# The half form of the attention step for two more chunks, loaded through the batch loader

## The chip, the cores and the metric

The kernel runs on one core of a Trainium2 chip. The metric is device time in microseconds of one execution. Three runs of the kernel before gave 206.95, 206.97 and 208.53 us; their median is 206.97.

The engines by the names of the profile: PE is TensorE (matmuls; PEld its weight loads), DVE is VectorE, ACT is ScalarE, POOL is GpSimd, SP is the engine that issues most DMAs here. Each executes its own instructions in order.

## The reference, cut to what matters

A recurrence of retention, 4 batches, 8 heads, 768 steps, head size 64, and behind it a feed-forward layer:

```python
# q, k, v: (4, 8, 768, 64); gamma[h] = 1 - 2**(-5-h); scale = 1/8
state = gamma * state + outer(k[t], v[t])
y[t]  = scale * q[t] @ state
x     = y as (3072, 512)            # tokens x (head, dim)
h     = maximum(x @ w_in, 0)        # w_in:  512 x 2048
out   = (h * h) @ w_out             # w_out: 2048 x 512
```

## The kernel before, in words

The 768 steps of a batch are cut into six chunks of 128, so there are 24 chunks, numbered m = 0 to 23; chunk 6 is the first of batch 1. Inside a chunk the recurrence is a masked product of scores, and between chunks a 64 x 64 state for each head is carried. The decay is put into q and k (or v) as powers of gamma, so that the mask is only a triangle.

The feed-forward layer takes the chunks in blocks: block 0 is chunks 0 to 3, then come ten blocks of two chunks. For a block, the first product (L803) makes 16 slices of h, ScalarE takes the relu (L812), and VectorE or ScalarE squares it; the second product is done with seven half-size products in place of eight (L837; for blocks 0 and 1 partly at L1096, and plainly at L1002). Block 2 needs the attention output of chunk 6 at place 51 and that of chunk 7 at place 55; block 3 begins at place 67.

TensorE's instruction stream is a list of "pieces" of the feed-forward work, each about 0.8 us, and before piece n the attention work that was `put` at place n is emitted. Places 16 to 31 are the plain second products of chunks 0 and 1 and the first products of block 1; places 32 to 50 the half-size products of chunks 2 and 3 and of block 1, seven matmuls a place; places 51 to 66 are block 2, and each later block has 16 places. Every engine's order follows from this list, that of the DMA queues on SP and POOL too.

There are three forms of the attention step. Chunks 0 to 3 use a form for pairs. The **full form** (`attend`, chunks 4 to 7 before) scales k by VectorE (`scale_k`), casts v on POOL (`cast_v`, L385), transposes q and k on TensorE (L399, L412) with copies out of PSUM on ScalarE (L405, L419), makes scores of 128 x 128 (L440) that VectorE masks (L447), a state (L479), and outputs (L508, L516). The **half form** (`attend2`, from chunk `PACK_FROM` on) lays a chunk out as two halves of 64 steps, the even heads on partitions 0 to 63 and the odd heads on 64 to 127. POOL casts k into a tile with zeros off the diagonal (`cast_k2`, L658, two instructions of 64 partitions). VectorE scales v by the decay (`scale_v2`, L667), and POOL copies it, again in two instructions, into a second tile with zeros off the diagonal (L675). q and k are transposed by DMA from SP (L425 for the q of two chunks, L681 for each k). The scores are eight matmuls of 64 columns (L697) with one mask on VectorE (L704); each half makes a state (L724), copied to SBUF by two ScalarE instructions (L733, L734); the outputs are up to 16 matmuls of 64 columns (L746, L753). The tiles `ks_bd2s` and `v_bd2s` are two each, and chunks take them in turn; `kT` tiles are two as well.

Loads: `load_q` (L105) brings the q of two chunks in one 512 KB DMA from SP. `load_kv` (L124) brings k or v of one chunk in one 256 KB DMA from SP with all 128 partitions. `batch_loads` (L147) is a generator that brings k or v of a batch in the layout of the half form, one DMA for each half of the partitions and each of four head pairs: 128 KB each on SP for chunks 8 to 11, 96 KB each (three chunks) on POOL for the later batches. All DMAs of SP go through one queue, and each waits for the one eight before it. The weights w_out are loaded and cast by POOL's DMAs (L171).

`attend2(m, d, before, q_at, qturn_at, k_at, turn_at, v_at)` puts the steps of a chunk: states at d-6 and d-3, scores at d-5, outputs at d; the others at the places given, for later chunks d-19, d-16, d-18, d-13 and d-9. `pack_constants` makes the decay table and the mask of the half form in two steps, and `zero_off_diagonal` clears tiles once on POOL.

Of the kernel before, what the change touches and what calls it, by code (L numbers as in the profile page):

```python
# [21 lines left out]

PACK_FROM = 8


@with_exitstack
def kernel(
# [9 lines left out]
    nc = tc.nc  # L39
# [13 lines left out]
    NCHUNK = len(chunks)  # L53
# [79 lines left out]
    def batch_loads(m, name, size):  # L133


        b, i = chunks[m]
        src, to = (k, raw_k) if name == "k" else (v, raw_v)
        t = kept_tiles.pop((m, name), None)
        if t is None:
            t = stage_tile(2 * NCH * NPAIR * D)  # L140
        t = t.rearrange("s (p w d) -> s p w d", p=NPAIR, d=D)
        for j in range(NCH - i):
            to[m + j] = t[:, :, 2 * j : 2 * j + 2].rearrange("s p u d -> s u p d")
        for w in range(0, NCH - i, size):
            for hh, rows in enumerate(halves):
                for p in range(NPAIR):
                    (nc.sync if m == 8 else nc.gpsimd).dma_start(  # L147
                        t[rows, p, 2 * w : 2 * (w + size)],
                        src[b, 2 * p + hh, (i + w) * C : (i + w + size) * C].rearrange(
                            "(w s) d -> s w d", s=64  # L150
                        ),
                    )
                    yield
# [41 lines left out]
    def exponents(pattern, step, name, logs, parts=(slice(0, P),)):  # L195
        ex_i = const.tile([P, NCH, H], I32, name=f"{name}_i")
        for rows in parts:
            nc.gpsimd.iota(ex_i[rows], pattern=pattern, base=0, channel_multiplier=step)

        def scaled():  # L200
            ex_f = const.tile([P, NCH, H], FP32, name=f"{name}_f")
            nc.vector.tensor_copy(ex_f[:], ex_i[:])
            nc.vector.tensor_tensor(
                out=ex_f[:],
                in0=ex_f[:],
                in1=logs[:, None, :].to_broadcast([P, NCH, H]),
                op=ALU.mult,
            )
            return ex_f

        return scaled
# [52 lines left out]
    def pack_constants():  # L264
        lng2 = const.tile([P, 2, NPAIR], FP32)
        for hh, rows in enumerate(halves):
            for p in range(NPAIR):
                nc.gpsimd.memset(lng2[rows, :, p : p + 1], float(np.log(gammas[2 * p + hh])))
        logs = lng2.rearrange("s u p -> s (u p)")
        scaled = exponents([[C, NCH], [C // 2, 2], [0, NPAIR]], 1, "ex_k2", logs, halves)  # L270
        nc.gpsimd.memset(cmask2[:], 0.0)
        for rows in halves:
            nc.gpsimd.affine_select(
                out=cmask2[rows],
                in_=cmask2[rows],
                compare_op=ALU.is_gt,
                fill=1.0,
                base=0,
                pattern=[[-1, 2], [-2, C // 4]],
                channel_multiplier=1,  # L280
            )
# [77 lines left out]
    at = {m: {} for m in range(NCHUNK)}  # L359
# [303 lines left out]
    def scale_v2(m):  # L663
        b, i = chunks[m]
        vn = raw_v.pop(m)
        v2 = v2pool.tile([P, 2 * NPAIR, D], BF16, name="v2")
        nc.vector.tensor_tensor(  # L667
            out=v2.rearrange("s (u p) d -> s u p d", u=2),
            in0=vn,
            in1=kf2[:, i, :, :, None].to_broadcast([P, 2, NPAIR, D]),  # L670
            op=ALU.mult,
        )
        v_bd = v_bd2s[m % 2]
        for hh, rows in enumerate(halves):
            nc.gpsimd.tensor_copy(v_bd[rows, :, hh, :], v2[rows])  # L675
        at[m].update(v2=v2, v_bd=v_bd)

    def transpose_k2(m):
        a = at[m]
# [535 lines left out]
    def put(place, what, *args):  # L1215
        parts.setdefault(place, []).append((what, args))
# [16 lines left out]

    def attend2(m, d, before, q_at, qturn_at, k_at, turn_at, v_at):
        if m % 2 == 0:
            put(q_at, scale_q, m, 0)
            put(q_at + 1, scale_q, m, 1)
            put(qturn_at, dma_transpose_q, m)
        put(k_at, cast_k2, m)
        put(v_at, scale_v2, m)  # L1240
        put(turn_at, transpose_k2, m)
        put(max(d - 6, before), state2, m, 0)
        put(d - 5, scores2, m)
        put(d - 3, state2, m, 1)
        put(d, outputs2, m)
# [7 lines left out]
    put(13, load_w_out, 1)  # L1253
    put(17, load_q, 6)
    attend(5, None, None, 17, 18, 18, (20, 21), 21, 23)
    for m, name in ((6, "k"), (6, "v"), (7, "k"), (7, "v")):
        put(18, load_kv, m, name)
    put(19, load_q, 8)
    put(19, load_w_out, 2)
    put(19, load_w_out, 3)  # L1260
    attend(6, (31, 32), 34, 33, 34, 35, (38, 39), 39, 42)
    attend(7, None, None, 37, 38, 40, (43, 44), 44, 47)

    def early_at(tb, c0, place, begin_at, at_places):
        held = []
# [18 lines left out]
    early_at(1, 0, 3, 32, (34, 34, 35, 36))  # L1284
    for place, tb, which in ((47, 0, 1), (49, 0, 0), (50, 1, 1), (52, 1, 0)):
        put(place, early_store, tb, which)
    packed = pack_constants()
    put(22, next, packed)
    put(38, next, packed)
    for j, t in enumerate(ks_bd2s + v_bd2s + [s_bds[2]]):  # L1290
        for hh in range(2):
            put(24 + j, zero_off_diagonal, t, hh)

    put(37, load_q, 10)
    done = [57, 62] + [70 + 8 * j for j in range(14)]

    ahead = {
        8: (36, 40, 43, 44, 47), 9: (0, 0, 45, 46, 53), 10: (50, 54, 55, 57, 60), 11: (0, 0, 60, 63, 68)
    }
    for m, d in zip(range(PACK_FROM, NCHUNK), done):  # L1300
# [70 lines left out]
```

## Time and profile before

| what | before |
|---|---|
| median of three runs | 206.97 us |
| time of the profiled execution | 208.36 us |
| its span, first to last instruction | 206.6 us |
| granted TensorE clock, mean | 0.998 |
| mean DMA rate over the span | 185 GB/s |
| q1 (DMAs from SP), share of 16 engines' span | 68.4% |
| q0 (DMAs from POOL), share | 19.2% |
| kT transposes (L681): count, us to landing, min / median / max | 16, 3.1 / 4.9 / 9.5 |
| qT transposes (L425): count, us to landing, min / median / max | 8, 3.3 / 5.8 / 9.3 |

An engine's busy time in the profile is the sum of its instructions; a line with "idle before" names who ended the wait. "SPq" is SP as an issuer of DMAs: its entry lasts as long as the issuing takes, which grows when the queue is full. The time to landing is counted from the issue. In the rows of digits, the span is cut into 40 slices of 5.2 us, and a digit is the busy share in tenths.

### The profile page before, as it was taken

The page shows a single profiled execution, that of the slowest core. Times are in us where ns is not written, and L with a number is a line of the kernel's source. Part 1 is how long each engine was busy: PE and PEld are TensorE (multiplying, and loading weights), DVE is VectorE, ACT ScalarE, POOL GpSimd, SP SyncE. Part 2 cuts the span into 40 slices and gives each one's busy share as a digit, 9 for nine tenths or more (in the row PEclk, how much of TensorE's full clock was granted, in tenths as well). Part 3 has the DMA queues.
Part 4 walks back from the last instruction along what each step waited for, and adds up shares of the span by engine and source line. Part 5 has one row for each costly group of instructions (what it writes and reads, how often), then busy time and mean ns, then how long its engine had stood idle before and what let it go on. Part 6 is the DMA issues. An engine that isn't in the chain of part 4 may idle for free.

```text
span 206.6 us, 5855 instructions
## 1 busy us (share of the span) xinstructions
PE 196.7 (95%) x2373; PEld 165.2 (80%) x2373; DVE 152.9 (74%) x305; ACT 135.6 (66%) x276; POOL 112.1 (54%) x198
## 2 busy tenths in 40 slices
PE   5889999999999999999999899999999999999993
PEld 1457644876888998789989699999989999898883
DVE  4687899498885678589697588598697797474374
ACT  8375885677943666693794595793785786874730
POOL 5332549823230768975999788779986226100000
PEclk9999999999999999999999999999999999999999
DMA  6999999999999999899699998799897551300202
GB/s 160 290 313 379 310 268 247 205 203 239 238 169 174 240 292 134 149 289 185 174 200 180 221 225 176 190 197 158 217 201 156 137 105 38 119 0 3 102 0 102
DMA packets 70730, 38.12 MB, mean 185 GB/s; under 512 B 43952, under 2 KB 64688, under 8 KB 70704
## 3 DMA queue, kind: packets, MB, share of 16 engines
q1 hardware_dynamic: 65520, 29.37, 68.4%
q0 software_dynamic: 5184, 8.39, 19.2%
q8 instruction: 18, 0.29, 0.6%
q14 instruction: 8, 0.07, 0.1%
HBM read 27.26 MB, written 6.29 MB: 162 GB/s over the span
## 4 chain that ended last, share of the span: by engine, by line
PE 69%; DMA 17%; POOL 4%; DVE 4%; ACT 2%; issue 1%; SPq 0%; DVEq 0%; ACTq 0%
PE psf L803 28%; PE psf L837 12%; PE tp L837 8%; DMA kT<-ks_bdp 7%; PE psf L1096 6%; DMA stage<-in_moe_w_in_dram 4%; DMA w_out_bf<-in_moe_w_out_dram 3%; PE psf L1002 3%; DMA kn<-in_k_dram 3%; POOL stage L147 2%; PE st L697 2%; POOL ks_bdp L658 2%; PE y L753 1%; PE y L746 1%; PE c_ps L724 1%
## 5 line engine op out<-in xcount | busy, mean ns | idle before, releaser
L803 PE MATMUL psf<-xt,w_in_bf 128*128 128x256 bf16 (+2 forms) x880 | 92.5, 259 | 0.4 <-DVE w_in_bf L336 0.3
L803 PEld LDWEIGHTS <-w_in_bf 128*128 128x128 bf16 x880 | 70.9, 98 | 11.2 <-DVE w_in_bf L336 0.7
L812 ACT ACTIVATE h<-psf 128x512 bf16<-128x512 f32 x96 | 56.2, 595 | 20.5 <-PE psf L803 20.0
L774 DVE TENSOR_TENSOR h<-h 128x512 bf16<-128x512 bf16 x72 | 31.8, 458 | 14.8 <-ACT h L812 14.6
L658 POOL CAST ks_bdp<-stage 64x512 bf16<-64x512 f32 x32 | 25.6, 799 | 20.6 <-issue 12.1
L675 POOL COPY v_bd<-v 64x512 bf16<-64x512 bf16 x32 | 20.6, 642 | 23.4 <-DVE v L667 22.2
L837 PEld LDWEIGHTS <-h 128*128 128x128 bf16 x288 | 26.3, 98 | 3.3 <-DVE h L774 0.6
L833 DVE TENSOR_TENSOR osb<-psf,u 128x256 f32<-128x256 f32 x34 | 13.7, 422 | 17.1 <-ACT u L878 9.9
L147 POOL DMA_DIRECT2D stage<-in_k_dram x32 | 21.0, 662 | 0.0
L147 POOL DMA_DIRECT2D stage<-in_v_dram x32 | 21.0, 662 | 0.0
L760 ACT ACTIVATE xt<-y 128x512 bf16<-128x512 f32 x16 | 12.0, 748 | 8.8 <-PE y L753 8.8
L366 DVE TENSOR_TENSOR qs<-qn,qf 128x512 bf16<-128x512 f32 x22 | 16.6, 758 | 1.1 <-DMA qn<-in_q_dram 1.1
L837 PEld LDWEIGHTS <-k_bd 128*128 128x128 bf16 x144 | 13.7, 98 | 1.8 <-issue 0.2
L772 ACT ACTIVATE h<-h 128x512 bf16<-128x512 bf16 x24 | 14.6, 626 | 0.5
L667 DVE TENSOR_TENSOR v<-stage,kf 128x512 bf16<-128x512 f32 x16 | 13.4, 838 | 0.0
L733 ACT ACTIVATE s_bd<-c_ps 64x256 bf16<-64x256 f32 x29 | 10.6, 367 | 3.4 <-PE c_ps L724 3.3
L704 DVE TENSOR_TENSOR pt<-st,cmask 128x512 bf16<-128x512 f32 x16 | 11.0, 687 | 2.4 <-PE st L697 1.9
L734 ACT ACTIVATE s_bd<-c_ps 64x256 bf16<-64x256 f32 x29 | 11.0, 378 | 0.4
L837 PE MATMUL tp<-w_out_bf,h 128*128 128x256 bf16 x72 | 11.2, 273 | 0.0
L334 POOL CAST w_in_bf<-stage 128x256 bf16<-128x256 f32 x14 | 6.1, 465 | 9.2 <-DMA stage<-in_moe_w_in_dram 9.2
L837 PE MATMUL psf<-w_sum,h 128*128 128x256 bf16 x72 | 10.8, 273 | 0.0
L833 DVE TENSOR_TENSOR k_bd<-h 128x512 bf16<-128x512 bf16 x18 | 10.4, 576 | 0.3
(146 smaller groups left out, 328.7 us busy)
## 6 DMA issues: line engine op xcount, KB each, us to landing
qn<-in_q_dram SPq DMA_DIRECT2D x12, 512.0 KB, 7.0
out_dram<-osb SPq DMA_DIRECT2D x23, 256.0 KB, 3.3
stage<-in_k_dram POOLq DMA_DIRECT2D x32, 96.0 KB, 4.5
stage<-in_v_dram POOLq DMA_DIRECT2D x32, 96.0 KB, 4.9
stage<-in_moe_w_in_dram SPq DMA_DIRECT2D x4, 512.0 KB, 6.9
stage<-in_moe_w_in_dram SPq DMA_DIRECT2D x2, 1024.0 KB, 10.9
w_out_bf<-in_moe_w_out_dram POOLq DMA_DIRECT2D x4, 512.0 KB, 9.5
kn<-in_k_dram SPq DMA_DIRECT2D x2, 512.0 KB, 6.4
```

The costliest lines, as they stand in the source:

```text
L147: (nc.sync if m == 8 else nc.gpsimd).dma_start(t[rows, p, 2 * w : 2 * (w + size)], src[b, 2 * p + hh, (i + w) * C : (i + w + size) * C].re ...
L366: engine.tensor_tensor(out=out, in0=by, in1=table[:, :, None].to_broadcast([P, H, D]), op=ALU.mult)
L658: nc.gpsimd.tensor_copy(ks[rows, :, hh, :].rearrange("s (u p) d -> s u p d", u=2), kn[rows])
L667: nc.vector.tensor_tensor(out=v2.rearrange("s (u p) d -> s u p d", u=2), in0=vn, in1=kf2[:, i, :, :, None].to_broadcast([P, 2, NPAIR, D]), ...
L675: nc.gpsimd.tensor_copy(v_bd[rows, :, hh, :], v2[rows])
L772: nc.scalar.activation(hv, hv, AF.Square)
L774: nc.vector.tensor_mul(hv, hv, hv)
L803: nc.tensor.matmul(hp, lhsT=w_in_bf[g][:, cb, fq * 128 : (fq + 1) * 128], rhs=xts[tb][:, cb, cols], start=(cb == 0), stop=(cb == NCB - 1),)
L812: nc.scalar.activation(hv, hp[:], AF.Relu)
L833: nc.vector.tensor_tensor(out=out, in0=in0, in1=in1, op=op)
L837: nc.tensor.matmul(to, lhsT=left[:, j], rhs=right(j) if callable(right) else right[:, j], start=(start and j == 0), stop=(stop and j == NF ...
L1096: nc.tensor.matmul(to[:], lhsT=left(j), rhs=right(j), start=(start and j == 0), stop=(j == NFB // 2 - 1), skip_group_check=True,)
```

## The change

Chunks 6 and 7 take the half form: `PACK_FROM` goes from 8 to 6, and their two `attend` calls and four `load_kv` are dropped. The k and v of chunks 6 to 11 now all come through `batch_loads` in 96 KB DMAs on SP, chunks 6 to 8 at places 18 to 21 and chunks 9 to 11 at places 32 to 40. The load of q for chunk 8 moves from place 19 to 24, that of 10 from 37 to 36. Constants and cleared tiles of the half form are made sooner. In `attend2` the POOL copies of v are a step of their own, one place behind the scaling, and the transposes of k go from d-13 to d-15. Some loads of chunks 12 to 17 on POOL are a few places later.

On SP the order up to chunk 9 is after the change: q of 6; eight k loads; eight v loads; q of 8; qT of 6; two output stores; kT of 6; eight k loads; q of 10; kT of 7; six v loads; qT of 8; two v loads; kT of 8; an output store; kT of 9. Before it was: q of 6; k, v of 6; k, v of 7; q of 8; five k loads; two output stores; three k loads; eight v loads; q of 10; qT of 8; kT of 8; kT of 9. For the later blocks SP's order is the same in both.

```diff
-PACK_FROM = 8
+PACK_FROM = 6
...
-                    (nc.sync if m == 8 else nc.gpsimd).dma_start(
+                    (nc.sync if m == PACK_FROM else nc.gpsimd).dma_start(
...
+        at[m]["v2"] = v2
+
+    def copy_v2(m):
         v_bd = v_bd2s[m % 2]
         for hh, rows in enumerate(halves):
-            nc.gpsimd.tensor_copy(v_bd[rows, :, hh, :], v2[rows])
-        at[m].update(v2=v2, v_bd=v_bd)
+            nc.gpsimd.tensor_copy(v_bd[rows, :, hh, :], at[m]["v2"][rows])
+        at[m]["v_bd"] = v_bd
...
         put(v_at, scale_v2, m)
+        put(v_at + 1, copy_v2, m)
...
-    for m, name in ((6, "k"), (6, "v"), (7, "k"), (7, "v")):
-        put(18, load_kv, m, name)
-    put(19, load_q, 8)
...
-    attend(6, (31, 32), 34, 33, 34, 35, (38, 39), 39, 42)
-    attend(7, None, None, 37, 38, 40, (43, 44), 44, 47)
...
+    put(24, load_q, 8)
     packed = pack_constants()
     put(22, next, packed)
-    put(38, next, packed)
+    put(27, next, packed)
     for j, t in enumerate(ks_bd2s + v_bd2s + [s_bds[2]]):
         for hh in range(2):
-            put(24 + j, zero_off_diagonal, t, hh)
-
-    put(37, load_q, 10)
-    done = [57, 62] + [70 + 8 * j for j in range(14)]
+            put(20 + j, zero_off_diagonal, t, hh)
+
+    put(36, load_q, 10)
+    done = [44, 49, 57, 62] + [70 + 8 * j for j in range(14)]
     ahead = {
-        8: (36, 40, 43, 44, 47), 9: (0, 0, 45, 46, 53), 10: (50, 54, 55, 57, 60), 11: (0, 0, 60, 63, 68)
+        6: (25, 28, 30, 32, 34), 7: (0, 0, 34, 36, 39),
+        8: (36, 40, 43, 44, 47), 9: (0, 0, 47, 48, 53), 10: (50, 53, 55, 56, 60), 11: (0, 0, 60, 63, 68)
     }
...
-                *ahead.get(m, (d - 19, d - 16, d - 18, d - 13, d - 9)))
+                *ahead.get(m, (d - 19, d - 16, d - 18, d - 15, d - 9)))
...
-        (8, "k"): [23, 23, 24, 24, 25, 32, 32, 33],
-        (8, "v"): [33, 33, 34, 34, 35, 35, 36, 36],
-        (12, "k"): [49, 50, 51, 52, 53, 54, 55, 56] + [74 + j for j in range(8)],
-        (12, "v"): [58, 59, 60, 61, 62, 64, 65, 66] + [82 + j for j in range(8)],
+        (6, "k"): [18 + j // 4 for j in range(8)] + [32 + j // 2 for j in range(8)],
+        (6, "v"): [20 + j // 4 for j in range(8)] + [37 + j // 2 for j in range(8)],
+        (12, "k"): [49, 50, 51, 52, 57, 58, 59, 60] + [74 + j for j in range(8)],
+        (12, "v"): [61, 62, 63, 64, 65, 66, 67, 68] + [82 + j for j in range(8)],
...
-        loads = batch_loads(m, name, 4 if m == 8 else 3)
+        loads = batch_loads(m, name, 3)
```

More of the change, by code (lines that the diff above doesn't have):

```diff
@@ L1286 @@
         put(place, early_store, tb, which)
+    put(24, load_q, 8)
     packed = pack_constants()
     put(22, next, packed)
-    put(38, next, packed)
+    put(27, next, packed)
     for j, t in enumerate(ks_bd2s + v_bd2s + [s_bds[2]]):
         for hh in range(2):
-            put(24 + j, zero_off_diagonal, t, hh)
-    put(37, load_q, 10)
-    done = [57, 62] + [70 + 8 * j for j in range(14)]
+            put(20 + j, zero_off_diagonal, t, hh)
+    put(36, load_q, 10)
+    done = [44, 49, 57, 62] + [70 + 8 * j for j in range(14)]
     ahead = {
-        8: (36, 40, 43, 44, 47), 9: (0, 0, 45, 46, 53), 10: (50, 54, 55, 57, 60), 11: (0, 0, 60, 63, 68)
+        6: (25, 28, 30, 32, 34), 7: (0, 0, 34, 36, 39),
+        8: (36, 40, 43, 44, 47), 9: (0, 0, 47, 48, 53), 10: (50, 53, 55, 56, 60), 11: (0, 0, 60, 63, 68)
     }
-    for m, d in zip(range(PACK_FROM, NCHUNK), done):
+    for m, d in zip(range(PACK_FROM, NCHUNK), done, strict=True):
         attend2(m, d, done[m - PACK_FROM - 1] if m > PACK_FROM else 0,
-                *ahead.get(m, (d - 19, d - 16, d - 18, d - 13, d - 9)))
+                *ahead.get(m, (d - 19, d - 16, d - 18, d - 15, d - 9)))
         if m >= 12 and m % 2 == 0:
```

## The prediction

> **What bounds it.** I read the page first, then the two waits tables, then the timelines of the tensor engine and of the SP queue. Busy times and the DMA row of the page:
>
> ```profile
> PE 196.7 (95%) x2373; PEld 165.2 (80%) x2373; DVE 152.9 (74%) x305; ACT 135.6 (66%) x276; POOL 112.1 (54%) x198
> DMA  6999999999999999899699998799897551300202
> ```
>
> TensorE is busy for 196.7 of 206.6 us. But the DMA row shows the 16 engines as full as TensorE until about 160 us: a transfer added there has no free room. What TensorE still waits for in mid-kernel is in its waits (engine and line, releaser: us in total, times, longest):
>
> ```profile
> PE st L697 <- DMA kT<-ks_bdp: 1.5, 2, 1.0
> ```
>
> L697 is the score product of the half form, and it waits for the DMA that transposes k. In the chain these are the stalls before 84.20 (0.46 us) and 115.47 (1.0 us). So the one transfer that the change adds for chunks 6 and 7 is the one TensorE already waits for. SP's timeline from 47 us (start, us taken, what):
>
> ```profile
> 47.19 4.34 SPq L147 DMA_DIRECT2D stage<-in_k_dram  x5
> 51.81 1.37 SPq L1013 DMA_DIRECT2D out_dram<-osb  x2
> 53.22 2.00 SPq L147 DMA_DIRECT2D stage<-in_k_dram  x3
> 55.32 6.27 SPq L147 DMA_DIRECT2D stage<-in_v_dram  x8
> 61.69 0.57 SPq L105 DMA_DIRECT2D qn<-in_q_dram  x1
> 62.36 3.13 SPq L425 DMA_TRANSPOSE qT<-qs  x1
> 65.59 2.85 SPq L681 DMA_TRANSPOSE kT<-ks_bdp  x2
> ```
>
> Each entry starts where the one before ended: SP issues without a gap, held back by the transfers themselves (0.78 us for a 128 KB load). The first kT here is chunk 8's; issued at 65.59, landed 5.0 us later by the DMA view, at 70.6. Its reader on TensorE:
>
> ```profile
> 71.79 0.40 PE L697 MATMUL st<-qT,kT 128*128 128x64 bf16 x8
> ```
>
> So the slack of chunk 8's keys is 1.2 us. That number decides the case.
>
> **TensorE's work.** Starts in its timeline give the lengths. Chunks 6 and 7 in the full form: q transposes 0.45, k transposes 2 x 0.22, scores 4 x 0.22, states 2 x 0.24, outputs 0.45 and 0.67; together 3.37 us. In the half form, from the rows of chunks 8 to 12: scores 2 x 0.23, states 4 x 0.12, outputs 0.35 (no state yet) and 0.46; together 1.75. The change saves **1.62 us** on the bound engine, all of it between 53 and 68 us.
>
> **The queue.** Bytes of q, k and v stay the same. Ahead of chunk 8's kT, SP has in both programs k and v of chunks 6 to 11, q of 8 and 10, two output stores and chunk 8's qT; after, it also has qT for 6 and kT for 6 and 7. Nothing that lay ahead of it moves behind it. A transpose costs, from below, its issue alone, 1.23 us (shortest row of L681); at the other end, 1.7 us, the seven quarter-microsecond slices in which the lone one issued at 173.4 moved bytes. I take 1.4: q of 10 landed at 61.69 + 5.6 = 67.3, and the three transposes behind it by 71.5. Three more are **4.2 us** (3.7 to 5.1). Chunk 8's kT would land at 70.6 + 4.2 = 74.8, and TensorE, 1.62 ahead, would want it at 70.2.
>
> The transposes' price can be set beside a page. The Trainium skill, "DMA: Bandwidth & Descriptors", section "Latency and other measured facts", gives 261 GB/s as the effective rate of a DMA transpose; an estimate by it is 1.0 us for 256 KB, so 3.0 us in place of 4.2, and a sum 1.2 us lower. The queue's own landings speak for the larger number.
>
> Where the wait falls, entry by entry:
> - **kT of 6.** SP reached the first two output stores at 51.81. Ahead of them lay 4 x 256 KB, q of 8 and 5 x 128 KB; after, it is 16 x 96 KB, q of 8 and qT of 6 (256 KB): 128 KB more, 0.8 us. Stores from 52.6, kT issued at 54.0 and landed at 59.0. The cast that it needs is no limit: POOL's memsets end at 42.6, and the keys land at about 48, when the same number of bytes had landed before (k of 7: 35.21 + 13.2). TensorE reaches the scores of chunk 6 (place 39) at 51.85 + 7 pieces x 0.77 + a state of 0.12 = 57.3. Wait: **1.7 us**.
> - **kT of 7** stands behind eight 96 KB loads (8 x 0.59 = 4.7 us, three quarters of the 0.78) and q of 10 (0.57 as issued here, up to 2 with the queue full). Issue 54.0 + 1.3 + 4.7 + 1.3 = 61.3, landing 66.3. TensorE is at its reader (place 44) five pieces, a score, two states and an output later: 59.0 + 4.7 = 63.7. Wait: **2.6 us**.
> - **kT of 8** stands behind six v loads, qT of 8, two v loads: 61.3 + 1.3 + 3.5 + 1.3 + 1.2 = 68.6, landing 73.6; by the whole queue above, 74.8. TensorE arrives at 66.3 + 7.2 (seven pieces, place 51, scores, states, an output) = 73.5. Wait: 0.1 to 1.3, taken as **0.8**.
>
> SP and TensorE are both in order: what stands behind each waiting score product is the whole dense product stream, so these waits add up.
>
> **What costs nothing.** The half-row 96 KB loads replace 256 KB loads of all rows: 12 more issues on SP, each at least 0.33 us (the shortest store issue), hidden while SP is held back by transfers anyway; uncovered, 4 us at most, 0 taken. POOL gets four casts of k (0.80 each) and four copies of v (0.64) for two casts of v: +4 us in a stretch (42.6 to 68) where it mostly waits. VectorE has five instructions fewer. ScalarE loses the copies of transposes (about 3.4 us) and gains eight state copies of 0.37. The scaling of v for chunk 6 and of q for 8 come at 54 to 56 us, about when their loads land; up to 0.5 us of VectorE waiting, which only delays osb sums with room behind them. Moving the k transposes from d-13 to d-15 changes nothing for chunks 12 on: SP's order stays q load, qT, kT, kT, two stores, and SP waits there for POOL's cast, not for its place. It is worth nothing.
>
> **What the late copies of v give.** Chunk 10's kT was issued at 78.40 when POOL's cast ended, and POOL had sat behind copies waiting for v and two loads (2 x 0.66). After, no load stands ahead of that cast, and the first stall (0.46) goes. The second stall, at 115.47, came from a transpose that took 9.5 us to land among POOL's loads; those remain. Bounds: both stay (0) or both go (1.5). I take 0.8.
>
> **Sum.** -1.6 + 1.7 + 2.6 + 0.8 - 0.8 = **+2.7 us**. The profiled execution had a span of 206.6 and a time of 208.36, 1.8 us around the span, near the highest of the three runs (208.53); the median is 206.97. The sum is a difference of spans, and I add it to the median: 206.97 + 2.7, rounded, is **209.6 us**, 1.3% slower. The unknown terms give this case 208.3 to 211.3: transposes at 3.7 to 5.1 us, stalls gone 0 to 1.5.
>
> **Rivals.**
> - *The queue has room* (ends faster). If transposes slip between loads, or the loads in half rows run faster, so that chunk 8's kT lands early enough for a TensorE that is 1.6 ahead, the work saved and the old stalls are pure gain: 206.97 - 1.6 - (0.5 to 1.5) gives 204 to 205. It decides where the three transposes together delay the queue by nothing. With a total of up to 2.8 us (1.2 of slack and 1.6 of work) the kernel is still no slower. For it: the DMA share is a mean and hides short gaps. Against: SP's issue alone is 1.23 us for each, without gaps. Chance 0.14.
> - *The waits only eat the gain.* Transposes at about 0.9 us, landing spacing of the fastest of the three, and kT of 6 hidden: 206 to 208.9. Chance 0.22, since kT's waits hang on landings of 3.1 to 9.5 us of which I used 5.0.
> - *The queue is worse than its rows.* The last two 256 KB loads of all rows landed at 48.4 and 49.3, so 0.45 us per 128 KB, and half-row loads take 0.78: for the 1 MB or so that moves after 46 us, 8 x 0.33 = 2.6 more. Or a transpose takes 9.5 us to land, as the one issued at 105.96, in place of 5.0. That is 211.3 to 214. Chance 0.14.
> - *The clock falls in a wait.* If the wait for kT of 7 grows past what this kernel has shown (longest 2.1 us, at the start, granted clock 0.99 or 1.00 in every stretch), TensorE could run the four pieces after it at half rate, 4 x 0.77 = 3.1 us more: 212.7. Chance 0.05.
>
> For the last: the Trainium skill, "TensorE: Matmul & The Clock Gate", Part 1, lets the clock drop to half after about 3.4 us of idleness; by that rule my wait of 2.6 stays short of it. No run here shows a drop.
>
> **Chances and range.** The forecast has 0.45, the rivals the rest. More than 1% either way (2.1 us, about what a measurement here tells from no change) is slower over 209.04 and faster under 204.90. Forecast and the two worse rivals give 0.64, less 0.07 for the forecast's lower edge (208.3 to 209.04): slower 0.57. Of the faster rival's 0.14, 0.13 lies below 204.90: faster 0.13; same 0.30. The range goes from 205.0 to 212.8: it leaves out most of the faster rival and the upper half of the third. The forecast's own range is 208.3 to 211.3.
>
> **What would show it.** Right: three waits of the score product for kT between 57 and 75 us, of 1 to 3 us each, some 5 us in total against 1.5; TensorE busy about 195 us and its span longer; SP without gaps from 30 to 70; chunk 8's scores at 73.5 to 75 rather than 71.79; later stretches shifted but of the same length. Wrong: kT of 6 landing before 57.3 or the score products of 6 and 7 without a wait (the first rival), a granted clock under 1.00 (the last), or waits of TensorE for VectorE or POOL rather than DMA, which I cost at nothing.

## The result, and the profile after

The changed kernel takes 217.36 us (median of six executions, 216.08 to 220.33); the kernel before, run beside it, 208.47 (six, 206.95 to 208.95). The ratio is 1.043 with a 95% interval of 1.038 to 1.049: 8.9 us more where 2.7 were forecast, and the forecast's range ended at 212.8. The sign was right, the size three times too small. (1.5 us of the gap between 209.6 and 217.36 are that the forecast stood on a median of 206.97 for the kernel before, and that kernel gave 208.47 in the six executions beside this one; and 206.97 + 2.7 is 209.7, not 209.6.) Times below are medians of all executions, and ratios leave out the disturbed, longer ones; where an experiment has no ratio, or its trace is longer than its median, the profiled execution was a disturbed one, of which only starts and waits up to 96 us are used (more of it only for the clock, at the end).

The profiled execution took 217.83 us, with a span of 216.1 against 206.6. Its busy times, granted clock and DMA row:

```profile
PE 196.4 (91%) x2361; PEld 164.4 (76%) x2365; DVE 152.6 (71%) x301; ACT 134.8 (62%) x277; POOL 116.1 (54%) x204
PEclk9999999999969999999999999999999999999999
DMA  6999999998999999999989999999699450500202
```

TensorE's busy time hardly moved (196.7 before): the work saved is offset by a stretch at half clock, and the additional time is idle time. The clock row has a dip that the kernel before lacks. The waits of TensorE (us in total, times, longest):

```profile
PE st L700 <- DMA kT<-ks_bdp: 9.2, 6, 3.0
...
PE psf L1005 <- DMA w_out_bf<-in_moe_w_out_dram: 1.3, 1, 1.3
...
PE psf L1099 <- ACT osb L1112: 0.3, 1, 0.3
```

L700 is the score product (L697 before): 9.2 us in six waits where there were 1.5 in two. TensorE's timeline shows them one by one (start, us, what, and in brackets the idle time just before): chunks 6, 7, 8, 10, 14 and 16.

```profile
61.92 0.61 PE L700 MATMUL st<-qT,kT 128*128 128x64 bf16 x8 [2.98 <-DMA kT<-ks_bdp]
...
70.27 0.41 PE L700 MATMUL st<-qT,kT 128*128 128x64 bf16 x8 [1.64 <-DMA kT<-ks_bdp]
...
78.58 0.41 PE L700 MATMUL st<-qT,kT 128*128 128x64 bf16 x8 [0.57 <-DMA kT<-ks_bdp]
...
92.80 0.41 PE L700 MATMUL st<-qT,kT 128*128 128x64 bf16 x8 [2.24 <-DMA kT<-ks_bdp]
...
124.22 0.41 PE L700 MATMUL st<-qT,kT 128*128 128x64 bf16 x8 [1.46 <-DMA kT<-ks_bdp]
...
139.70 0.41 PE L700 MATMUL st<-qT,kT 128*128 128x64 bf16 x8 [0.34 <-DMA kT<-ks_bdp]
```

SP's timeline, to be set beside the one of before (the issue of chunk 8's kT is the 74.19, which was 65.59):

```profile
30.65 13.77 SPq L147 DMA_DIRECT2D stage<-in_k_dram  x8
44.59 7.84 SPq L147 DMA_DIRECT2D stage<-in_v_dram  x8
52.54 0.55 SPq L105 DMA_DIRECT2D qn<-in_q_dram  x1
53.21 2.45 SPq L425 DMA_TRANSPOSE qT<-qs  x1
55.75 0.99 SPq L1016 DMA_DIRECT2D out_dram<-osb  x2
56.84 1.29 SPq L684 DMA_TRANSPOSE kT<-ks_bdp  x1
58.19 6.13 SPq L147 DMA_DIRECT2D stage<-in_k_dram  x8
64.36 0.61 SPq L105 DMA_DIRECT2D qn<-in_q_dram  x1
65.08 2.27 SPq L684 DMA_TRANSPOSE kT<-ks_bdp  x1
67.40 3.95 SPq L147 DMA_DIRECT2D stage<-in_v_dram  x6
71.47 1.27 SPq L425 DMA_TRANSPOSE qT<-qs  x1
72.79 1.27 SPq L147 DMA_DIRECT2D stage<-in_v_dram  x2
74.19 1.27 SPq L684 DMA_TRANSPOSE kT<-ks_bdp  x1
```

There is no gap: SP is the bound of this stretch. The first eight 96 KB loads take 1.72 us each (13.77 / 8), the next 0.98 (7.84 / 8), later ones 0.77 and 0.66; no group reaches the 0.59 of the forecast. SP comes to the output stores at 55.75 where the forecast had 52.6, so kT of 6 is issued at 56.84 and not at 54.0.

The span, term by term, from matched starts in TensorE's two timelines:

| term | us |
|---|---|
| TensorE's work for chunks 6 and 7 | -1.62 |
| waits for kT of 6, 7, 8: 2.98 + 1.64 + 0.57 (none before) | +5.19 |
| half clock behind the first of them | +1.52 |
| waits for kT of 10, 14, 16: 2.24, 1.46, 0.34 (before 0.46, 1.02, 0) | +2.56 |
| place 32 reached at 53.31, not 51.85, most of it a wait for w_out (1.3 us, L1005) | +1.46 |
| a wait for an output sum (L1099) | +0.29 |
| sum, against 9.5 measured | +9.40 |

The loss at place 32 lies ahead of the first step that the change adds to TensorE. The wait for w_out was anywhere between nothing and 1.74 us in the traces of kernels of before (none in e5, 0.16 in e7, 1.74 in e1, where it ended at 36.85, ahead of the first added transpose at 53.56), and between nothing (e6) and 1.44 us (e10) in those of kernels of after. So it comes and goes without the change. But the change's loads are on SP from 30.65 us on, and no run parts a share of theirs from this scatter: that the change has no part in it is not shown.

### The profile page after: what moved, and what is told of

It reads as the page before. It is cut to its first block, busy times and chain, and to the rows that moved or that the text cites. A ratio compares the mean times of both kernels' runs of the same rounds, so it can differ in the third digit from the quotient of the medians.

```text
span 216.1 us, 5866 instructions
## 1 busy us (share of the span) xinstructions
PE 196.4 (91%) x2361; PEld 164.4 (76%) x2365; DVE 152.6 (71%) x301; ACT 134.8 (62%) x277; POOL 116.1 (54%) x204
## 4 chain that ended last, share of the span: by engine, by line
PE 44%; DMA 17%; POOL 4%; DVE 2%; issue 1%; DVEq 0%
PE psf L806 21%; DMA kT<-ks_bdp 17%; PE psf L840 10%; PE tp L840 7%; POOL stage L147 2%; PE st L700 2%; POOL ks_bdp L658 1%; PE y L756 1%; PE y L749 1%; PE psf L1099 1%; PE c_ps L727 1%; POOL v_bd L678 1%; DVE osb L836 1%; DVE u L836 1%; DVE v L667 0%
## 5 line engine op out<-in xcount | busy, mean ns | idle before, releaser
L658 POOL CAST ks_bdp<-stage 64x512 bf16<-64x512 f32 x36 | 28.2, 782 | 32.9 <-issue 14.5
L678 POOL COPY v_bd<-v 64x512 bf16<-64x512 bf16 x36 | 23.9, 664 | 22.9 <-DVE v L667 19.0
L707 DVE TENSOR_TENSOR pt<-st,cmask 128x512 bf16<-128x512 f32 x18 | 12.4, 688 | 14.2 <-PE st L700 14.0
L763 ACT ACTIVATE xt<-y 128x512 bf16<-128x512 f32 x18 | 13.5, 747 | 9.2 <-PE y L756 9.2
L366 DVE TENSOR_TENSOR qs<-qn,qf 128x512 bf16<-128x512 f32 x22 | 17.3, 794 | 1.1 <-DMA qn<-in_q_dram 1.1
L736 ACT ACTIVATE s_bd<-c_ps 64x256 bf16<-64x256 f32 x33 | 12.1, 368 | 6.9 <-PE c_ps L727 6.8
L700 PE MATMUL st<-qT,kT 128*128 128x64 bf16 x144 | 7.4, 196 | 9.2 <-DMA kT<-ks_bdp 9.2
L667 DVE TENSOR_TENSOR v<-stage,kf 128x512 bf16<-128x512 f32 x18 | 15.0, 832 | 0.0
L700 PEld LDWEIGHTS <-kT 128*128 128x128 bf16 x144 | 6.3, 99 | 10.9 <-DMA kT<-ks_bdp 10.6
L737 ACT ACTIVATE s_bd<-c_ps 64x256 bf16<-64x256 f32 x33 | 12.5, 378 | 0.5
L334 POOL CAST w_in_bf<-stage 128x256 bf16<-128x256 f32 x14 | 6.6, 499 | 8.9 <-DMA stage<-in_moe_w_in_dram 8.9
L836 DVE TENSOR_TENSOR k_bd<-h 128x512 bf16<-128x512 bf16 x18 | 10.7, 597 | 0.3
```

The costliest lines, as they stand in the source:

```text
L366: engine.tensor_tensor(out=out, in0=by, in1=table[:, :, None].to_broadcast([P, H, D]), op=ALU.mult)
L658: nc.gpsimd.tensor_copy(ks[rows, :, hh, :].rearrange("s (u p) d -> s u p d", u=2), kn[rows])
L667: nc.vector.tensor_tensor(out=v2.rearrange("s (u p) d -> s u p d", u=2), in0=vn, in1=kf2[:, i, :, :, None].to_broadcast([P, 2, NPAIR, D]), ...
L678: nc.gpsimd.tensor_copy(v_bd[rows, :, hh, :], at[m]["v2"][rows])
L700: nc.tensor.matmul(st[:, c, :], lhsT=kT[:, c, :], rhs=half_of(a["qT"], p, u), start=True, stop=True,)
L836: nc.vector.tensor_tensor(out=out, in0=in0, in1=in1, op=op)
```

## The experiments

Kernels called "of before" start from the kernel before, the others from the kernel after. Ratios are against the kernel before, run on the same chip. Kernels whose queue is the same up to kT of 8 issue it within 1 or 2 us of each other (73.33 in e6 to 74.99 in e4, 74.19 after; 65.32 in e7, 65.59 before), so differences between single traces below hold to about 1 us.

**e1: three more transposes in the kernel of before.** It transposes weights into tiles that nobody reads.

```diff
+    def extra_transpose():
+        spare = kTpool.tile([P, 2 * NPAIR, C], BF16, name="kT")
+        nc.sync.dma_start_transpose(spare[:], w_in_bf[0][:, 0:2, :].rearrange("s c f -> s (c f)"))
+    for place in (28, 32, 36):
+        put(place, extra_transpose)
```

> The kernel before, with three DMA transposes added on SP that nobody reads (of a finished weight tile, 256 KB each, at places 28, 32 and 36, where the changed kernel has qT of 6, kT of 6 and kT of 7); all else as before, the full form for chunks 6 and 7 included. Theory A, the three transposes fill the queue: the kT of chunk 8 lands 3.7 to 5.1 us later than 70.6, so its score product, at 71.79 before, starts at 74 to 76, and the kernel is 2.5 to 5 us slower than before. Rival B, the half-row loads of 96 KB make the queue slower: this kernel keeps the old loads, so it stays within 1 us of before and the score product of chunk 8 starts at 72.

Measured: 217.11 us, ratio 1.044 (1.035 to 1.054), as much as the whole change and about twice the 2.5 to 5 us that theory A gave. SP's timeline (L1296 are the added ones) shows what they took there:

```profile
53.56 2.14 SPq L1296 DMA_TRANSPOSE kT<-w_in_bf  x1
...
56.89 1.50 SPq L1296 DMA_TRANSPOSE kT<-w_in_bf  x1
...
65.39 2.04 SPq L1296 DMA_TRANSPOSE kT<-w_in_bf  x1
...
72.88 3.44 SPq L681 DMA_TRANSPOSE kT<-ks_bdp  x2
```

2.14 + 1.50 + 2.04 is 5.7 us, 1.9 each and not 1.4. Chunk 8's kT is issued 7.3 us later than in the kernel before, of which 1.45 were there when SP began with the loads of chunk 8 (48.64 against 47.19); 5.84 are left. TensorE's waits for a late v, kT of 8 and kT of 10 sum to 2.60 + 0.90 + 2.11, and the half clock came here too, for 6.83 us. The span of e1, 8.5 us longer than before, adds up much as that of after does: 1.5 at place 32, 3.5 for the waits at chunk 8, 2.6 for the half clock and 1.65 more at chunk 10, less the 1.0 of the wait at chunk 14, which is not there.

**e5: the same three as plain copies.** In e1's place a plain copy within SBUF of as many bytes, in 1024 pieces of 256 bytes, again unread.

```diff
-        nc.sync.dma_start_transpose(spare[:], w_in_bf[0][:, 0:2, :].rearrange("s c f -> s (c f)"))
+        nc.sync.dma_start(
+            spare.rearrange("s u c -> s (u c)").rearrange("s (j c) -> s j c", c=C),
+            w_in_bf[0].rearrange("s c f -> s (c f)")[:, 0 : 16 * C].rearrange("s (j c) -> s j c", c=2 * C)[:, :, 0:C],
+        )
```

> The kernel before with three plain DMA copies where the first experiment had three transposes: the same 256 KB of a finished weight tile, in 1024 pieces of 256 bytes, from SBUF to the same tile in SBUF, on SP at the same places. Theory A1, a DMA transpose stands for itself: in the traces nearly nothing moves for about 1 us before each one (49 and 70 packets a microsecond in the first experiment where 600 to 1000 is usual), so it drains what is ahead of it, and a plain copy of the same size does not; this kernel is then at most 3 us slower than before. Theory A2, any 256 KB in small pieces fills the full queue as much: it is as slow as the first experiment, 8 us or more over before.

Measured: 217.33 us (213.83 to 219.76). The shortest of the four executions, the only undisturbed one, is 5.6 us over the kernel before: more than the 3 that theory A1 allows, less than the 8 of A2, so the time does not decide for A2. SP's timeline:

```profile
53.30 0.66 SPq L1296 DMA_DIRECT2D kT<-w_in_bf  x1
...
71.35 2.98 SPq L681 DMA_TRANSPOSE kT<-ks_bdp  x2
```

A copy occupies SP for 0.66 us only, but chunk 8's kT is still issued 5.76 us late, of which 0.37 were there before the loads of chunk 8 (47.56 against 47.19): 5.39 us, 1.8 each, against e1's 1.95. The time appears at the loads behind the copies. So in the queue 256 KB in small pieces cost about as much when they are only copied, and theory A1, that transposing is what costs, falls; whether fewer and larger pieces would be cheaper, no run shows. The Trainium skill ("DMA: Bandwidth & Descriptors", section "Latency and other measured facts") has 261 GB/s for a DMA transpose with a non-contiguous middle dimension; the forecast set an estimate of 1.0 us by it against 1.4. Both fall short of the 1.95 here; of the 1.35 that e2 shows below, only the estimate does.

**e2: the three transposes taken out of the kernel after.** q of 6 and k of 6 and 7 are transposed on TensorE, with a copy on ScalarE.

```diff
+    def pe_transpose_k2(m):
...
+        for c in range(2 * NPAIR):
+            nc.tensor.transpose(tp[:, c, :], a["ks"][:, c].rearrange("s hh d -> s (hh d)"), ident[:])
+        nc.scalar.activation(kT[:], tp[:], AF.Copy)
...
-            put(qturn_at, dma_transpose_q, m)
+            put(qturn_at, transpose_q if m == 6 else dma_transpose_q, m)
...
-        put(turn_at, transpose_k2, m)
+        put(turn_at, pe_transpose_k2 if m < 8 else transpose_k2, m)
```

> The changed kernel, with q of 6 and k of chunks 6 and 7 transposed by TensorE (8 matmuls and one ScalarE copy each) and not by DMA; the loads are those of the changed kernel. TensorE has 3 x 0.45 us more than the changed kernel, 0.27 less than the kernel before. Theory A: the waits for kT of 6 and 7 go, kT of 8 lands about 4 to 5 us earlier than in the changed kernel, and the time is that of before, -1 to +2 us (208 to 211 by the median of before of 208.5). Rival B: the loads still hold kT of 8 back by 3 us or more, and the time stays over 212.

Measured: 213.7 us, ratio 1.020 (1.010 to 1.030). The waits at chunks 6 and 7 are gone; TensorE is at chunk 8 early and waits there. SP's and then TensorE's timeline:

```profile
70.14 1.25 SPq L684 DMA_TRANSPOSE kT<-ks_bdp  x1
```

```profile
76.50 0.61 PE L709 MATMUL st<-qT,kT 128*128 128x64 bf16 x8 [4.58 <-DMA kT<-ks_bdp]
```

Without one added transpose, kT of 8 is issued at 70.14, 4.05 before the kernel after and still 4.55 behind the kernel before. So in the kernel after the three transposes cost 4.05 (1.35 each, the forecast's price), and some 4.5 us are left for the loads, for which it had taken nothing. Both halves of what was expected are there: theory A's 4 to 5 us, and rival B's 3 us or more.

**e11: smaller loads in the kernel of before.** Only the loads of chunks 8 to 11 are cut, 32 of 64 KB for 16 of 128.

```diff
-        loads = batch_loads(m, name, 4 if m == 8 else 3)
+        loads = batch_loads(m, name, 2 if m == 8 else 3)
```

> The kernel before with the k and v of chunks 8 to 11 loaded in 32 DMAs of 64 KB where it has 16 of 128 KB: the same bytes, halves and pieces of 256 bytes. If the loads go by bytes, 0.39 us each on SP, the kT of 8 is issued within 1 us of 65.59 and the time is that of before. If a DMA costs 0.66 to 0.98 us nearly whatever it holds (as the 96 KB loads of the changed kernel took, against 0.78 for 128 KB before), the kT of 8 is issued 8 us or more later and the kernel is over 4% slower.

Measured: 218.1 us, ratio 1.049 (1.042 to 1.057), from cutting loads alone. SP's timeline:

```profile
47.29 7.35 SPq L147 DMA_DIRECT2D stage<-in_k_dram  x10
...
60.61 11.37 SPq L147 DMA_DIRECT2D stage<-in_v_dram  x16
...
76.30 2.69 SPq L681 DMA_TRANSPOSE kT<-ks_bdp  x2
```

11.37 / 16 is 0.71 us for 64 KB; the same rows of before give 0.78 for 128 KB. Taken one by one, without the few that are held up, the issues differ even less: their median is 0.615 us for 64 KB here, 0.625 for 96 KB after and 0.633 for 128 KB before. kT of 8 is issued 10.7 us late. That SP and not the DMA engines sets this pace is to be seen in a window of four microseconds (columns: window, length, busy time and count of PE, PEld, DVE, ACT, POOL, then clock, DMA share, GB/s), first e11, then the kernel before:

```profile
58.00:62.00 4.00, 3.53 (x42) 2.94 (x41) 3.86 (x9) 1.51 (x5) 0.00 (x0) 1.00 0.37 82
```

```profile
58.00:62.00 4.00, 3.91 (x50) 3.33 (x48) 3.34 (x7) 2.01 (x6) 1.83 (x3) 1.00 0.92 165
```

The engines are busy for 0.37 where they were for 0.92, and the small v loads land 2.6 us after their issue, so that at 0.71 each fewer than four are under way. The Trainium skill ("DMA: Bandwidth & Descriptors", section "Issuing engines are not separate DMA queues") calls the time that a sequencer needs to start a DMA usually small against the DMA itself; for these loads it was the limit.

**e13 and e14: larger loads.** The other direction: 16 loads of 192 KB for the 32 of 96 KB. e14 has e2's edit as well.

```diff
-        loads = batch_loads(m, name, 3)
+        loads = batch_loads(m, name, 6 if m == 6 else 3)
...
-        (6, "k"): [18 + j // 4 for j in range(8)] + [32 + j // 2 for j in range(8)],
-        (6, "v"): [20 + j // 4 for j in range(8)] + [37 + j // 2 for j in range(8)],
+        (6, "k"): [18 + j // 4 for j in range(8)],
+        (6, "v"): [20 + j // 4 for j in range(8)],
```

> The kernel after, with k and v of chunks 6 to 11 in 16 loads of 192 KB (each all six chunks of one pair of heads and one half of the partitions, at places 18 to 21) in place of 32 of 96 KB. Same bytes, everything else in the same order. Theory N (a load costs SP about 0.7 us whatever it holds, as 64, 96 and 128 KB did): kT of 6 is issued about where it is after (56.8), kT of 7 some 3 us behind it, kT of 8 by 66; the waits for kT of 7 and 8 go, and the time falls by 2 to 6 us against the kernel after, to 211 to 215. Theory B (the price goes with the bytes, 0.7 us for each 96 KB, and the dear 64 KB loads had another reason): the 16 loads take 1.4 us each, kT of 6 is issued near 68 with a wait of some 12 us, and kT of 8 no sooner than after (74); the time is 219 to 226.

> The same 16 loads of 192 KB, and q of 6 and k of 6 and 7 transposed on TensorE, so that SP carries none of the three added transposes. Theory N: kT of 8 is issued by 63, earlier than before the change (65.6), no wait for it, and the time is 205 to 209. Theory B: the loads of v of 6 and 7 come late, TensorE waits there for several us, kT of 8 is issued at about 70 as with 96 KB loads, and the time is 213 or more.

Measured: 220.93 us, ratio 1.060 (1.054 to 1.067), and 218.01, ratio 1.037 (1.024 to 1.049): e13 is slower than the same kernel with 96 KB (1.043), e14 by its median (e2 1.020; the intervals overlap). SP's and TensorE's timelines of e13:

```profile
31.02 19.01 SPq L147 DMA_DIRECT2D stage<-in_k_dram  x8
50.19 8.75 SPq L147 DMA_DIRECT2D stage<-in_v_dram  x8
...
69.63 1.45 SPq L425 DMA_TRANSPOSE qT<-qs  x1
```

```profile
64.44 0.37 PE L727 MATMUL c_ps<-v,ks_bdp 128*128 128x64 bf16 x4 [7.65 <-DVE v L667]
```

A 192 KB load takes 1.09 us (8.75 / 8): neither the 0.7 of theory N nor the 1.4 of theory B. So from 64 to 128 KB a load takes SP some 0.7 us whatever it holds, and at 192 KB it takes longer. By 71.08 SP has issued all that the kernel after has issued by 74.06, just before kT of 8; with SP's loads starting at 31.02 and 30.65 that is 3.35 us for 16 fewer loads, 0.2 each. The kernel loses all the same, since large loads put six chunks ahead of the first one's v: its state product waits 7.65 us. e14 waits 3.27 us for POOL's cast of k (at 55.88) and 4.08 for v (at 65.61).

So the 8.6 us by which kT of 8 comes later are 4.1 to 5.8 for the transposes (e2, e1) and the rest, 2.8 to 4.5, is by subtraction for more and smaller loads. The two can't be parted more sharply, as the price of each depends on how full the queue is beside it.

**e3: is it the clock?** Idle products keep TensorE busy ahead of the scores of chunk 6; their results are not used.

```diff
+    put(39, keep_awake, 14, 4 * C, ps_y, "y")
+    put(39, end_awake)
```

> The changed kernel with 14 idle matmuls of 512 columns (3.0 us at the full clock) on TensorE directly before the scores of chunk 6, so that it computes through the 2.98 us in which it waits for kT of 6. The granted clock, 0.50 from 62 to 65 us in the changed kernel, should stay at 1.00. If the halved clock costs what it takes (about 1.5 us), the kernel is 1.5 us faster than the changed one. If the end of the stretch is set by the queue (kT of 7 lands at 70.2 whatever TensorE does before it), TensorE reaches the scores of chunk 7 earlier, waits there about 1.5 us longer, and the time is the same within 0.7 us. I expect the second.

Measured: 216.57 us, ratio 1.042 (1.034 to 1.049), the same as after. The wait at chunk 6 is down to 0.43 and the clock stays whole there, but kT of 7 is then waited for 2.76 us, and the half clock comes there. A TensorE that is sooner only waits longer for the queue. The profiled execution thus moved the half clock and did not remove it; but another execution of e3 had a mean granted clock of 1.000, so no such stretch, and took 216.10 us, where two others with 0.991 and 0.984 took 216.14 and 217.00. So the half clock is part of the accounting, but not what sets the time.

**e4: the late copies of v.** The copies of v go back beside the scaling and the transposes of k back to d-13; all else as after.

```diff
-        put(v_at + 1, copy_v2, m)
+        put(v_at, copy_v2, m)
...
-                *ahead.get(m, (d - 19, d - 16, d - 18, d - 15, d - 9)))
+                *ahead.get(m, (d - 19, d - 16, d - 18, d - 13, d - 9)))
```

> The changed kernel with two of its parts undone: the copies of v at the place of the scaling again, and the transposes of k at d-13 for chunk 12 on. Theory: both parts cost and give nothing, the time is that of the changed kernel within 1 us, and the waits for the kT of chunks 10, 14 and 16 (2.24, 1.46 and 0.34 us in the changed kernel) remain. Rival C: the late copies are what makes these waits longer than before (0.46, 1.02 and none), and undoing them gives 2 us back.

Measured: 219.51 us, ratio 1.047 (1.036 to 1.059): no difference from after that these runs can tell. The wait for kT of 10 is 3.78 us here and 2.24 after, so the moved copies don't make it longer.

**e9: q of 12 out of the way of kT of 10.** After, kT of 10 stands directly behind the 512 KB load of q for chunk 12.

```diff
-            put(d - 33, load_q, m)
+            put(57 if m == 12 else d - 33, load_q, m)
```

> The changed kernel with one load moved: q of chunk 12 (512 KB on SP) from place 53 to 57, so that it stands behind the kT of chunk 10 and not directly ahead of it (it was issued at 82.59, that kT at 83.79 in the changed kernel; before, at 71.66 and 78.40). If the bunch of transfers still queued at 80 us makes the wait for kT of 10 (2.24 us, 0.46 before), that wait falls to 1 us or less and the kernel is 1 to 2 us faster than the changed one. If POOL's cast or its loads make it, nothing changes.

Measured: 216.65 us, ratio 1.041 (1.035 to 1.047). The wait for kT of 10 is gone, as expected; waits of 0.74 at chunk 12, 0.59 at 14 and 1.35 at 16 are there, and the time is that of after. The late waits come to 2.68 us in place of 4.04: the collision makes a part of them, not the whole.

**e6 and e7: halves in turn.** Consecutive loads alternate between the two halves of the partitions, in the kernel after (e6) and before (e7), to see whether loads into the same half hold each other up.

```diff
-            for hh, rows in enumerate(halves):
-                for p in range(NPAIR):
+            for p in range(NPAIR):
+                for hh, rows in enumerate(halves):
```

> The changed kernel with one edit in the batch loader: of the DMAs of a batch, the two halves of the partitions come in turn for each head pair, where the changed kernel issues the four DMAs of the lower half and then the four of the upper. Theory H, loads of one half keep only some of the 16 DMA engines busy (a mean of 7 to 11 between 50 and 54 us, 400 to 600 packets a microsecond): the eight v loads, 7.84 us on SP in the changed kernel, take 5 to 6 us, kT of 8 is issued 2 to 4 us earlier than 74.19, and the kernel is 2 to 4 us faster than the changed one. Rival L, a DMA costs SP its 0.7 to 0.9 us whatever it holds: no difference beyond 1 us.

> The kernel before with that same edit of the batch loader alone (halves in turn). Theory H: the eight v loads of 128 KB, 6.27 us on SP before, become shorter by 1 us or more, the kT of chunks 10 and 14 land earlier and the waits of 0.46 and 1.02 us shrink: 0 to 1.5 us faster than before. Rival L: no difference.

Measured: e6 217.06 us, ratio 1.034 (1.022 to 1.046), which overlaps that of after; e7 208.28, ratio 0.998 (0.992 to 1.003). The order of the halves makes no difference that these runs can tell.

**e8: all transposes ahead of the loads of chunks 9 to 11.** These loads go to places 37 to 44, q of 10 to place 45.

```diff
-    put(36, load_q, 10)
+    put(45, load_q, 10)
...
-        (6, "k"): ... + [32 + j // 2 for j in range(8)],
-        (6, "v"): ... + [37 + j // 2 for j in range(8)],
+        (6, "k"): ... + [37 + j // 2 for j in range(8)],
+        (6, "v"): ... + [41 + j // 2 for j in range(8)],
```

> The changed kernel with SP's order changed and nothing added or left out: the loads of chunks 9 to 11 (places 32 to 40) move to 37 to 44 and the load of q for chunk 10 from 36 to 45, so that kT of 7 stands directly behind kT of 6. Theory A, the sum of the queue sets the end: the wait for kT of 7 (1.64 us) goes, kT of 8 is issued within 2 us of 74.19, TensorE waits there for what it no longer waits before, and the time is that of the changed kernel within 1.5 us. Rival O, the order is the fault: the kernel is 3 us or more faster than the changed one.

Measured: 220.55 us, ratio 1.055 (1.045 to 1.065). The wait for kT of 7 goes, those for 6 (3.75) and 8 (2.63) are there, and later ones appear. The order in the queue moves the waits: for kT they sum to 8.9 us, where they summed to 9.2. The median is 3.2 us above that of after, more than the 1.5 that theory A allowed, though the intervals overlap; so this order is no better, and may be worse.

**e10 and e12: as much off SP as is easy.** e10 is e2 with k of 8 on TensorE as well; e12 adds e9's edit.

```diff
-        put(turn_at, pe_transpose_k2 if m < 8 else transpose_k2, m)
+        put(turn_at, pe_transpose_k2 if m < 9 else transpose_k2, m)
```

> The second experiment (q of 6, k of 6 and 7 transposed by TensorE) with k of chunk 8 transposed by TensorE too; loads as in the changed kernel. TensorE works 0.45 us more than there and 0.2 us more than before. There the one long wait was 4.58 us for kT of 8 and then 6.8 us at half the clock. If that wait was the whole of its loss, the score product of 8 starts at 72 to 73 and the kernel is within 1% of before. If the slower loads show up at the next reader (v of 8 or kT of 9), a wait of 2 us or more appears there and the kernel stays 2% slower.

> The last two changes together: q of 6 and k of 6, 7 and 8 on TensorE, and q of 12 loaded at place 57. If the waits for kT were all that the half form lost, none over 1 us is left, and the kernel is within 1% of before, at best 1 us faster (the wait of 0.46 us for kT of 10 gone, 0.2 us more work).

Measured: e10 215.36 us, ratio 1.0235 (1.0125 to 1.0345); e12 212.87, ratio 1.0105 (1.0003 to 1.0207). In e10 the scores of 8 run without a wait at 72.95, and chunks 10 and 14 wait instead (1.93 and 2.98 us); in e12 chunk 10 doesn't wait either, 12 waits for 0.42, and 14 still does for 2.24, against the expectation that no wait over 1 us would be left. With four transposes off the queue and q of 12 out of the way the change is almost made good, but no version here beats the kernel before.

## Why the prediction was wrong, point by point

- **What bounds it** was read rightly: SP's queue, full from 30 to 74 us, releases each score product, and the waits are where they were forecast. The first rival, room in the queue, is refuted: every product that could have gained from it waits.
- **TensorE's work, -1.62**: right, and worth nothing: whatever TensorE gains ahead of a queue that is late it spends waiting (e2's 4.58 us at chunk 8, e3's shift of the wait from 6 to 7).
- **Three transposes, +4.2 (3.7 to 5.1)**: 4.05 in the kernel after (e2), 5.84 in the kernel before (e1). Within the bounds by the one, over them by the other.
- **Loads in half rows at nothing**: this step failed. The forecast named the price if the cover was gone, 4 us at most, and took 0 because "SP is held back by transfers anyway". But a 96 KB load took SP 0.66 to 0.98 us (the first eight 1.72) and not three quarters of a 128 KB load; e11 shows why the proportion doesn't hold: below 128 KB the time stays at about 0.7. The loads cost some 2.8 to 4.5 us of queue, and the three kT were issued at 56.84, 65.08 and 74.19, where the forecast had 54.0, 61.3 and 68.6. The third rival named this price, but from 256 KB loads against half rows, which is not what the runs showed.
- **The three waits, 1.7 + 2.6 + 0.8 = 5.1**: measured 2.98 + 1.64 + 0.57 = 5.19. The sum is right partly by luck. kT of 8 landed at 78.5, 3.7 us after the forecast's latest 74.8, and its wait is small only because TensorE was later too: 1.46 us at place 32, 1.3 more at chunk 6 and half a clock. So the queue time that the loads took is in the span under those terms, not in this sum.
- **Late copies give -0.8 (bounds 0 to -1.5)**: wrong in sign. The waits at chunks 10, 14 and 16 grew by 2.56 us. The copies themselves do nothing that can be told (e4). kT of 10 was waited for longer since it was issued at 83.79 behind q of 12 and took 9.0 us to land, where it had taken 5.8; with that collision removed, 2.68 us of late waits in place of 4.04 are still there, at chunks 12, 14 and 16 (e9). The step that failed is "later stretches shifted but of the same length": they were longer. This is the largest wrong term: 3.4 us. That the queue's delay is what makes them longer fits e9 and e12, but no run shows it by itself.
- **Nothing for POOL, VectorE and ScalarE**: held. POOL is busy 4.0 us longer (112.1 to 116.1), as forecast, and no new wait of TensorE is for one of them but 0.3 us at L1099 and 0.3 at L440, ahead of place 32.
- **The clock, chance 0.05**: it happened, behind the wait for chunk 6, and cost 1.5 us. The forecast set the length of its wait against a length of idleness ("my wait of 2.6 stays short of it"); the window behind the wait of 2.98, with the columns as above, shows half clock:

```profile
61.60:65.00 3.40, 3.08 (x21) 2.34 (x22) 1.72 (x3) 0.38 (x1) 0.97 (x2) 0.51 1.16 162
65.00:66.00 1.00, 1.00 (x14) 0.91 (x13) 0.00 (x0) 0.52 (x2) 0.70 (x2) 1.00 0.77 134
```

The clock is halved for about 3.4 us. The condition failed, not only the chance: what counts in these runs is how busy TensorE is in a fixed window, not how long it waits (last section). (The forecast's "No run here shows a drop" overlooks that the kernel before is at half clock too, though only from 205.67 us, behind its last matmul.)

No rival alone reaches 217: what happened is the forecast's own case together with the third rival's dear loads and the fourth's clock, which had been given separate chances as if one excluded the other. From +2.7 to +9.4: 3.4 for the late waits, 1.5 for the clock, 1.5 for the loss at place 32 that is not shown to be the change's, 0.3 for the output sum and 0.1 in the three waits. What stays open: why the late waits come at all, that at chunk 14 being anywhere from nothing (e1) to 3.0 us (e10), and why e1's transposes alone and e11's loads alone each cost as much as the whole change, so that the parts don't add up. A queue that is the bound passes on whichever part is late last, and the parts hide one another; that reading fits e2 and e11, but was not tested by itself.

## What to carry to other kernels

When a trace shows an issuing engine without a gap, price each added DMA by the queue's slope (time per entry where the queue is full) and not by its bytes or its issue alone; cutting loads into smaller ones is not free, and here below 128 KB a load's time on SP did not fall with its size. Work taken off the busiest engine is worth nothing in a stretch where a queue, not that engine, is last. And carry a delay forward to the next places where the old kernel already waited: here, chunks 10 and 14, they were the first to wait longer.

## What the runs showed of the hardware that was not expected

- A load of 256-byte pieces into 64 partitions occupies SP for about 0.7 us whether it has 64 KB (0.71), 96 KB (0.66 at the fastest) or 128 KB (0.67 for the fastest three of before); at 192 KB it takes 1.09. Held up by what is ahead of it in the queue, a 96 KB load took up to 1.72 (mean of the first eight after).
- A DMA transpose of 256 KB and a plain copy within SBUF of 256 KB in 256-byte pieces delay a full queue about alike: 5.84 and 5.39 us for three.
- The length of a wait does not tell whether the clock is halved: it was behind waits of 2.04 (e5), 2.24 (e12) and 2.76 us (e3), but not behind 2.24 (after, chunk 10), 2.43 (e6) and 3.75 us (e8, chunk 6). The traces show what does. In each of the 16 the changes of clock lie whole multiples of 3.413 us apart, so there is a fixed grid of windows of that length, which starts at another place in each execution. From 20 to 200 us, 788 of its windows were at full clock. All 18 in which TensorE was busy for up to 0.41 of the window were followed by half clock, and none of the others, busy for 0.42 or more, was. Such windows from after (chunks 6 and 10), e12 and e8 (two), columns as above:

```profile
58.14:61.55 3.41, 0.80 (x9) 0.47 (x5) 1.91 (x3) 0.83 (x3) 0.77 (x1) 1.00 1.26 203
88.86:92.27 3.41, 1.70 (x19) 1.29 (x16) 1.21 (x4) 2.23 (x5) 3.31 (x7) 1.00 1.20 227
```

```profile
114.37:117.78 3.41, 1.24 (x18) 1.15 (x19) 0.94 (x3) 0.60 (x2) 3.19 (x5) 1.00 1.17 209
```

```profile
57.13:60.55 3.42, 1.58 (x18) 1.19 (x15) 2.70 (x5) 1.13 (x4) 1.51 (x2) 1.00 1.47 263
60.55:63.96 3.41, 1.49 (x20) 1.37 (x21) 0.98 (x2) 0.24 (x1) 0.00 (x0) 1.00 0.77 170
```

TensorE is busy for 0.23 and 0.50 of its window after, 0.36 in e12, and 0.46 and 0.44 in e8, where the wait of 3.75 us is split between two windows; only the 0.23 and the 0.36 are followed by half clock. The Trainium skill ("TensorE: Matmul & The Clock Gate", Part 1) states an idle window of about 3.4 us that runs freely. The grid of 3.413 us agrees; that a wait must last as long does not hold here, and a wait from about 2 us on (2.04, e5) has to be counted as one that may halve the clock, by where it falls.
